# First-layer sums and stores handed out over the next pair, weight chunks asked for by ScalarE, one second-layer sum a step sooner, in a fused hash-attention and MLP kernel

## The chip, the cores and the metric

The kernel runs on one core of one Trainium2 chip. TensorE (PE) multiplies, VectorE (DVE), ScalarE (ACT) and GpSimd (POOL) do the rest, and SyncE (SP) mostly asks for transfers. The metric is the device time of the one core in microseconds (us), the median of a few runs. All sizes are fixed and all tensors float32 inside.

## The reference

Attention over buckets (a query sees the keys with the same six hash bits), followed by an MLP with a sigmoid GELU. What the change touches is the MLP alone.

```
q, k, v: (4, 8, 768, 64)   proj: (64, 6)   w_in: (512, 2048)   w_out: (2048, 512)
attn = softmax(where(bucket(q) == bucket(k), q k^T / 8, -1e9)) v
x = attn as (3072, 512)
h = x @ w_in
out = (h * sigmoid(1.702 h)) @ w_out
```

## The kernel before

**Stages.** Attention comes first (up to about 317 us of the profiled execution); it leaves `xT`, the transposed input of the MLP, in on-chip memory. Then comes the first layer (about 316 to 617 us), then the second (about 617 us to the end). Both layers are multiplied by a seven-product scheme: each operand is cut in 2 x 2 quarters, DVE and POOL form sums of the quarters (`sums_a` for the weights, `sums_b` for the data), PE makes seven products in place of eight, and the results are added up.

**First layer.** Tokens go in three blocks `sb` of 1024, features in eight tiles `mt` of 128 in each half, so there are 24 steps `n = 8 sb + mt`. One step makes four results of 128 features by 512 tokens, called `u`, `v`, `c21`, `c22`. A product (`product`, L740) is two multiplications by 128x128 weights over 512 columns; the trace shows each as two passes, so a product is "x4". Steps 0, 1, 20, 21, 22 and 23 run alone (`hidden`). Steps 2 to 19 run as nine pairs `t` (`pair_of_steps`), in which products 2 and 3 are themselves cut in seven smaller ones over 256 columns (`nested`, L801): PE makes a small product, DVE adds it to its result (L750), and the small products of one kind share a PSUM tile, so PE waits for DVE's addition before it goes on in that tile. The small products of the second kind (`third`) are left over to the start of the next pair (`behind`, `old`).

**What a step leaves.** ACT applies the GELU (`emit`, L747), and `g_outer` lets POOL form four sums of the results (L219 to L222 in `sums_b`; the second overwrites `v`). Seven tiles go to memory (`keep`, L744, 256 KB each: `c22`, `c21`, `u`, the overwritten `v` and the sums `t1`, `t2`, `t4`, which have one buffer each). In a pair, `g_outer` of both steps is called when the last nested results of the pair are done, that is after the product `p5(0)` of the next pair. In `hidden` it is called at the end of the step.

**Weights.** `w_out` comes as 64-bit numbers, and the chip makes float32 of them in chunks of 512 KB (`convert`): a transfer into `raw` (L162), six operations of DVE (L180, L182, L188, L193, L195, L198) and one of ACT (L190). `raw` has one buffer; L193 is its last reader. `conversions` strings 18 such chunks (two late ones of `w_in`, 16 of `w_out`) together; each call of `next(steps)` does one operation. `todo` gives each step of the first layer six calls, and in a pair they hang on the places 1 to 10 between the products (`hook`): the first step's at 1, 2, 2, 3, 3, 4, the second's at 6, 7, 7, 9, 9, 10.

**Order.** PE, DVE, ACT and POOL run their instructions in the order of the code (`ORDERED`). SP's order is made by a scheduler from the same code. All transfers before are asked for by SP, in one queue: one that waits for its data holds up all behind it. The instructions wait for each other by semaphores; a transfer also waits until the eighth one before it has landed.

**Second layer.** 21 steps of seven small products each, with `raw_g` or `s_in` as the data read back (L1013); DVE forms the sums for the next step (`later_sums`: L219, L220, L221, L222) at given places (`after(0)` to `after(4)`) of this one. At the step before the last another list is set at `after(3)`, which holds `later_sums[2:3]` too.

Of the kernel before, what the change touches and what calls it, by code (L numbers as in the profile page):

```python
# [8 lines left out]
F32 = mybir.dt.float32  # L9
# [10 lines left out]
P = 128  # L20
# [18 lines left out]
def kernel(  # L39
# [17 lines left out]
    nc = tc.nc  # L57
# [167 lines left out]
    XT = 512  # L225
# [469 lines left out]
    def feed_forward(tag, late=()):  # L695
# [9 lines left out]
        with ExitStack() as fctx:  # L705
# [12 lines left out]
            todo, turn = {}, [-1]  # L718
# [31 lines left out]
                nc.vector.tensor_tensor(dst, x, y, op=Alu.add)  # L750

            def g_outer(sb, mt, c11, c12, c21, c22):
                t1, t2, t4 = (stage.tile([P, XT], F32, tag=x, name=x, bufs=1) for x in ("t1", "t2", "t4"))
                for f, kept in zip(sums_b(nc.gpsimd, c11, c12, c21, c22, t1, t2, t4), ((4, t1), (1, c12), (5, t2), (6, t4))):
                    f()
                    keep(sb, mt, *kept)


            W = {}
# [69 lines left out]
            def pair_of_steps(t, mid):  # L829

                sb, m0 = divmod(2 * t, MT)
                mts = (m0, m0 + 1)
                a, b, u, v, c22, c21 = ([None, None] for _ in range(6))

                def p1(i):
                    a[i], u[i] = outer.tile([P, XT], F32, tag="a", name="product"), staged("u")
                    product(a[i], sb, mts[i], 1)
                    nc.scalar.copy(u[i], a[i])

                def p6(i):  # L840
                    product(a[i], sb, mts[i], 6, False)
                    v[i] = staged("v")
                    nc.scalar.copy(v[i], a[i])  # L843

                def p7(i):
                    product(a[i], sb, mts[i], 7, False)
                    c22[i] = staged("c22")
                    nc.scalar.copy(c22[i], a[i])

                def p5(i):  # L850
                    b[i] = outer.tile([P, XT], F32, tag="b", name="product")
                    product(b[i], sb, mts[i], 5)
                    add(v[i], b[i], v[i])

                def corner(i):
                    add(c22[i], b[i], c22[i])
                    emit(c22[i])
                    keep(sb, mts[i], 3, c22[i])

                def p4(i):  # L860
                    product(a[i], sb, mts[i], 4, False)
                    c21[i] = staged("c21")
                    emit(c21[i], a[i])
                    keep(sb, mts[i], 2, c21[i])

                def done2(i):
                    emit(u[i])
                    keep(sb, mts[i], 0, u[i])

                def done3(i):  # L870
                    emit(v[i])
                    if i == 0:
                        for j in range(2):
                            g_outer(sb, mts[j], u[j], v[j], c21[j], c22[j])

                def old():
                    if behind:
                        behind.pop(0)()

                def hook(at):  # L880
                    for f in mid.get(at, []):
                        f()

                p1(0)
                old()
                hook(1)
                p1(1)
                old()
                yield
                hook(2)  # L890
                p6(0)
                old()
                hook(3)
                p6(1)
                old()
                hook(4)
                p5(0)
                old()
                second = nested(2, sb, t, u, done2)
                second[0]()  # L900
                hook(5)
                p7(0)
                corner(0)
                second[1]()
                hook(6)
                p7(1)
                second[2]()
                hook(7)
                p5(1)
                corner(1)  # L910
                second[3]()
                hook(8)
                p4(0)
                second[4]()
                hook(9)
                p4(1)
                second[5]()
                third = nested(3, sb, t, v, done3)
                third[0]()
                behind.extend(third[1:])  # L920
                hook(10)

            heads = {}
# [7 lines left out]
            def hidden(sb, mt, mid=(), end=()):  # L931
                n = sb * MT + mt
                first = n not in heads
                nesting[0] = n < 2
                a, u = heads.pop(n) if n in heads else head(n)

                def old():
                    if behind:
                        behind.pop(0)()

                old()
                b = bank()
                if first:
                    product(b, sb, mt, 5)
                    old()
                product(a, sb, mt, 6, False)
                v, c21, c22 = (staged(x) for x in ("v", "c21", "c22"))
                nc.scalar.copy(v, a)
                if first:
                    old()  # L950
                    heads[n + 1] = head(n + 1)
                    old()
                else:
                    product(b, sb, mt, 5)
                product(a, sb, mt, 7, False)
                old()
                nc.scalar.copy(c22, a)
                add(c22, b, c22)
                emit(c22)
                keep(sb, mt, 3, c22)  # L960
                c = bank()
                product(c, sb, mt, 2)
                add(u, c, u)
                emit(u)
                keep(sb, mt, 0, u)
                if not first and n + 1 < n1 * MT and (n + 1) // 2 not in NESTED:
                    heads[n + 1] = head(n + 1)
                for x in mid:
                    x()
                product(a, sb, mt, 4, False)  # L970
                emit(c21, a)
                keep(sb, mt, 2, c21)
                product(b, sb, mt, 3, False)
                add(v, b, v)
                emit(v)
                g_outer(sb, mt, u, v, c21, c22)
                for x in end:
                    x()

# [114 lines left out]

            def conversions(cv, psum, chunks):

                gens = [convert(cv, *x, psum=psum) for x in chunks]
                next(gens[0])
                for i, x in enumerate(gens):
                    for y in gens[i + 1 : i + 2]:  # L1100
                        next(y)
                    for _ in x:
                        yield
                    yield

            def on(i, *fs):
                hooks[i] = hooks.get(i, []) + list(fs)
# [14 lines left out]
            order = [8 * k + 4 * c + i for c in range(2) for k in range(2) for i in range(4)]  # L1122
            chunks = [(w_out_sb[:, :, fc, :].rearrange("p r x -> p x r"), wo[fc]) for fc in order]
            steps = conversions(cv, cps, late + chunks)
            free = [i for i in range(LATE + 1, 3 * MT) if i % MT != MT - 1]
            for i in (list(range(1, LATE + 1)) if late else []) + free[:FC]:
                todo[i] = [lambda: next(steps)] * 6
# [13 lines left out]
                      [xT[:, k, XT * j : XT * (j + 1)] for k, j in ((2, 1), (0, 3), (1, 3), (1, 1))]]  # L1141
            places = [[x[:, j * TH : (j + 1) * TH] for x in y for j in range(2)] for y in places]
            more = nest_x(0, places[0])
            hidden(0, 1, nest_w(1) + more[2], more[3] + todo.pop(1, []))
            yield
            small_ctx.close()
            inner_ctx = fctx.enter_context(ExitStack())
# [2 lines left out]
            for t in NESTED:  # L1150
                sb, at = divmod(t, MT // 2)
                hooks = {}
                if at == 0:
                    on(1, x_sums[3], more[2][0])
                    for i, f in zip((2, 4, 5, 6, 7, 8, 9), more[2][1:] + more[3]):
                        on(i, f)
                for n, places_of in ((2 * t, (1, 2, 2, 3, 3, 4)), (2 * t + 1, (6, 7, 7, 9, 9, 10))):
                    x = todo.pop(n, [])
                    for i in places_of:
                        on(i, *x[:1])  # L1160
                        x = x[1:]
                    on(5 if n % 2 == 0 else 10, *x)
                if t + 1 < MT // 2:
                    on(5, *in_sums(t + 1))
                    on(8, *nest_w(t + 1))
                elif t + 1 == MT // 2:
                    on(5, *nest_w(0))
                if at == MT // 2 - 1:
                    x_sums = sums_b(nc.vector, *quarters_x(sb + 1))
                    more = nest_x(sb + 1, places[sb + 1])  # L1170
                    for i in range(3):
                        on(8 + i, x_sums[i])
                whole(pair_of_steps(t, hooks))
                yield
# [21 lines left out]
            for n, (sb, o) in enumerate(steps_out):  # L1196
# [11 lines left out]
                def after(at):  # L1208
# [1 line left out]
                        while pending:  # L1210
                            pending.pop(0)()

                    steps = [later_sums[at : at + 1]] if n == 0 else [[], later_sums[0:1], later_sums[1:2], later_sums[2:], []][at : at + 1]

                    if n + 2 >= len(steps_out):
                        turns = [lambda q=q: turned(m, int(final), int(not final), q, q + 1) for q in range(4)]
# [82 lines left out]
```

## Time and profile before

| | us |
|---|---|
| three runs | 884.53, 882.37, 883.58 (median 883.58) |
| profiled execution, its own time | 883.3 |
| its span from the first to the last instruction | 881.4 |
| PE busy | 855.8 |
| DVE busy | 709.9 |
| ACT busy | 340.6 |
| POOL busy | 330.8 |

The granted TensorE clock was 0.995 of full speed over the span. The page divides the span into 40 slices; PE is at 9 tenths or more in nearly all of them, so its few idle stretches have to be looked for one by one. In the timeline a row gives start, duration, engine, line, operation, output and inputs, and in brackets the idle time of that engine before it and what ended it. The list of waits gives, for an engine's line and what it waited for, the sum, the count and the longest. A view by windows gives each engine's busy time in each stretch.

### The profile page before, as it was taken

Reading aid. Unit: us, or ns where it says so; the run is one execution under the profiler, and the core shown is the slowest. Engines: PE = TensorE matmul, PEld = TensorE weight load, DVE = VectorE, ACT = ScalarE, POOL = GpSimd, SP = SyncE. Lnnn points to the kernel's source line nnn. Section 1 sums busy time; section 2 is a strip of 40 time slices with the busy share of each in tenths; the row PEclk is TensorE's granted clock in tenths of the full one; section 3 lists DMA queues with packets and bytes.
Section 4 is the critical chain, followed back from the end, with each engine's and each line's share of the span. In section 5 each row is a group of like instructions: output and inputs, shape, how many; then the busy total and the mean of one; then the engine's idle time right before and its main releaser. Section 6 shows DMA issues by size and latency. Waiting matters only on the chain.

```text
span 881.4 us, 13702 instructions
## 1 busy us (share of the span) xinstructions
PE 855.8 (97%) x4953; PEld 517.1 (59%) x4953; DVE 709.9 (81%) x1056; ACT 340.6 (39%) x567; POOL 330.8 (38%) x291
## 2 busy tenths in 40 slices
PE   9999999999999998999998899999999999999996
PEld 4444444444444443455554455544878888888885
DVE  4589999999999877767965687856797977897786
ACT  5866677766677632433333333333000000000000
POOL 4242243332234476377632254779913100000000
PEclk9999999999999999999999999999999999999998
DMA  6646644565542105354555555558745585477524
GB/s 132 95 62 106 94 83 84 102 115 98 94 82 81 35 21 194 120 176 146 199 184 171 198 192 191 177 205 310 246 184 191 177 226 215 155 225 237 196 99 99
DMA packets 169163, 132.12 MB, mean 150 GB/s; under 512 B 123616, under 2 KB 138112, under 8 KB 163712
## 3 DMA queue, kind: packets, MB, share of 16 engines
q1 hardware_dynamic: 166528, 129.70, 51.7%
q10 hardware_dynamic: 2560, 1.46, 0.7%
q8 instruction: 41, 0.67, 0.3%
q14 instruction: 34, 0.28, 0.1%
HBM read 79.69 MB, written 50.33 MB: 148 GB/s over the span
## 4 chain that ended last, share of the span: by engine, by line
PE 36%; issue 6%; DVE 5%; POOL 5%; DMA 1%; SPq 0%; ACT 0%; ACTq 0%; POOLq 0%; DVEq 0%
PE product L1058 26%; PE product L740 9%; PE small L801 2%; DVE xT L1062 1%; POOL t L222 1%; POOL t L221 1%; DMA raw<-in_moe_w_out_dram 1%; POOL t L219 1%; POOL v L220 1%; DVE v L750 1%; DVE y L1038 1%; DVE w_out_sb L195 0%; DVE v L1062 0%; DVE t2a L221 0%; DVE raw_g L220 0%
## 5 line engine op out<-in xcount | busy, mean ns | idle before, releaser
L433 ACT ACTIVATE e<-ps 128x768 f32<-128x768 f32 x192 | 151.2, 812 | 25.7 <-PE ps L432 23.1
L432 PE MATMUL ps<-qT,kT 64*128 64x384 f32 x768 | 155.1, 482 | 0.0
L465 PE MATMUL av<-e,v 128*32 128x385 f32 x1536 | 128.0, 487 | 0.0
L440 POOL TENSOR_TENSOR acc<-e 128x768 f32<-128x768 f32 x32 | 51.8, 1618 | 193.6 <-ACT e L433 174.1
L740 PE MATMUL product<-xT,w_in_sb 128*128 128x512 f32 x216 | 102.0, 602 | 3.6 <-ACT v L843 3.6
L465 PEld LDWEIGHTS av<-e,v 128*32 128x32 f32 x1536 | 48.6, 109 | 76.2 <-issue 74.5
L432 PEld LDWEIGHTS ps<-qT,kT 64*128 64x128 f32 x768 | 68.0, 187 | 38.5 <-issue 38.4
L740 PE MATMUL product<-t_x,s_in 128*128 128x512 f32 x192 | 89.4, 593 | 0.2 <-ACT u L928 0.2
L219 POOL TENSOR_TENSOR t<-v,u 128x512 f32<-128x512 f32 x24 | 33.6, 1399 | 110.9 <-ACT v L747 104.5
L1071 ACT COPY u<-product 128x256 f32<-128x256 f32 x21 | 7.8, 372 | 174.1 <-PE product L1058 140.8
L740 PEld LDWEIGHTS product<-xT,w_in_sb 128*128 128x128 f32 x216 | 41.3, 192 | 40.3 <-issue 33.7
L432 PE MATMUL ps<-qf,kf 64*128 64x384 bf16 x384 | 62.9, 324 | 0.1
L441 POOL TENSOR_TENSOR acc<-acc,e 128x768 f32<-128x768 f32 x32 | 55.8, 1744 | 2.5
L740 PEld LDWEIGHTS product<-t_x,s_in 128*128 128x128 f32 x192 | 36.3, 190 | 31.7 <-issue 27.5
L446 DVE SCALAR_TENSOR_TENSOR acc<-e 128x768 f32<-128x768 f32 x32 | 47.7, 1489 | 5.1 <-ACT e L433 5.1
L740 PE MATMUL product<-t_x,w_in_sb 128*128 128x512 f32 x96 | 45.3, 594 | 0.0
L432 PEld LDWEIGHTS <-kf 64*128 64x128 bf16 x384 | 18.9, 94 | 35.1 <-DMA q<-in_q_dram 6.2
L448 DVE TENSOR_TENSOR acc<-acc,e 128x768 f32<-128x768 f32 x32 | 34.3, 1072 | 3.3
L448 DVE TENSOR_TENSOR acc<-acc,acc 128x768 f32<-128x768 f32 x32 | 31.7, 991 | 6.3 <-POOL acc L441 3.2
L1058 PE MATMUL product<-raw_g,xT 128*128 128x256 f32 x152 | 35.1, 379 | 0.0
L221 POOL TENSOR_TENSOR t<-c,t 128x512 f32<-128x512 f32 x24 | 35.0, 1457 | 0.0
L222 POOL TENSOR_TENSOR t<-c,t 128x512 f32<-128x512 f32 x24 | 34.2, 1427 | 1.9
(241 smaller groups left out, 1636.9 us busy)
## 6 DMA issues: line engine op xcount, KB each, us to landing
raw_g<-g_dram SPq DMA_DIRECT2D x22, 1024.0 KB
s_in<-g_dram SPq DMA_DIRECT2D x20, 1024.0 KB
g_dram<-t SPq DMA_DIRECT2D x72, 256.0 KB
g_dram<-c SPq DMA_DIRECT2D x48, 256.0 KB
raw<-in_moe_w_in_dram SPq DMA_DIRECT2D x16, 512.0 KB
raw<-in_moe_w_out_dram SPq DMA_DIRECT2D x16, 512.0 KB
v<-in_v_dram SPq DMA_DIRECT2D x32, 192.0 KB
g_dram<-u SPq DMA_DIRECT2D x24, 256.0 KB
```

The lines of the kernel that those rows point to most:

```text
L219: return [lambda: eng.tensor_tensor(t1, b12, b11, op=Alu.subtract), lambda: eng.tensor_tensor(b12, b22, b12, op=Alu.subtract), lambda: eng ...
L221: lambda: eng.tensor_tensor(t2, b22, t1, op=Alu.subtract),
L222: lambda: eng.tensor_tensor(t4, b21, t2, op=Alu.subtract)]
L432: nc.tensor.matmul(ps[:, j, 0:HS], a[hs, keys], m[hs, cols], start=not last, stop=last)
L433: nc.scalar.activation(es[c][:, kt, :, 0:HS], ps[:, :, 0:HS], Act.Exp, scale=1.0 / D**0.5)
L440: nc.gpsimd.tensor_tensor(acc, es[c][:, 0, :, 0:HS], es[c][:, 1, :, 0:HS], op=Alu.add)
L441: nc.gpsimd.tensor_tensor(acc, acc, es[c][:, 2, :, 0:HS], op=Alu.add)
L446: nc.vector.scalar_tensor_tensor(acc, e[0], T * TINY, e[1], op0=Alu.add, op1=Alu.add)
L448: nc.vector.tensor_tensor(acc, acc, x, op=Alu.add)
L465: nc.tensor.matmul(av[D * j + d : D * j + d + 32, :], vt[:, t, j, d : d + 32], es[c][:, t, j, :], start=(t == 0), stop=(t == T - 1))
L740: nc.tensor.matmul(ps, wq[LEFT[i]][:, kc, :], xq[RIGHT[i]][:, kc, :], start=(start and kc == 0), stop=(kc == K2 - 1), skip_group_check=not ...
L1058: nc.tensor.matmul(ps, wq[LEFT[i]][:, c, :], gq[RIGHT[i]][:, c, :], start=(c == 0), stop=(c == F4 - 1))
```

## The change

Four things are edited.

1. In the first layer `g_outer` no longer runs the four sums and their stores at once: it puts four parts in a list, `outer_sums`, and `some(count)` runs that many of them. In a pair `some` stands behind the nested steps, 1, 2, 1, 2, 1 and 1 parts; in `hidden` all that is left runs before the fourth product, and the step's own four at its end. `c21` gets its buffer later in `hidden`.
2. The chunks are asked for with `queue=nc.scalar`, so by ScalarE, in its own order, and the request for the next chunk stands behind the fourth operation (L193) of this one.
3. In a pair the second step's six operations hang on 6, 7, 7, 7, 9, 9 in place of 6, 7, 7, 9, 9, 10; in step 1 four of the six stand before the fourth product.
4. In the second layer the third of `later_sums` (L221) moves from `after(3)` to `after(2)`.

```diff
             def g_outer(sb, mt, c11, c12, c21, c22):
-                t1, t2, t4 = (stage.tile([P, XT], F32, tag=x, name=x, bufs=1) for x in ("t1", "t2", "t4"))
-                for f, kept in zip(sums_b(nc.gpsimd, c11, c12, c21, c22, t1, t2, t4), ((4, t1), (1, c12), (5, t2), (6, t4))):
-                    f()
-                    keep(sb, mt, *kept)
+                t = {}
+                def part(i):
+                    if i != 1:
+                        t[i] = stage.tile([P, XT], F32, tag=f"t{i}", name=f"t{i}", bufs=1)
+                    sums_b(nc.gpsimd, c11, c12, c21, c22, t.get(0), t.get(2), t.get(3))[i]()
+                    keep(sb, mt, (4, 1, 5, 6)[i], t.get(i, c12))
+                outer_sums.extend(lambda i=i: part(i) for i in range(4))
+
+            outer_sums = []
+            def some(count):
+                for _ in range(count):
+                    if outer_sums:
+                        outer_sums.pop(0)()
...
                 second[0]()
+                some(1)
                 hook(5)
...
                 second[1]()
+                some(2)
                 hook(6)
...
                 second[2]()
+                some(1)
                 hook(7)
...
                 second[3]()
+                some(2)
                 hook(8)
...
                 second[4]()
+                some(1)
                 hook(9)
...
                 behind.extend(third[1:])
+                some(1)
                 hook(10)
...
-                v, c21, c22 = (staged(x) for x in ("v", "c21", "c22"))
+                v, c22 = staged("v"), staged("c22")
...
+                some(len(outer_sums))
                 for x in mid:
                     x()
+                c21 = staged("c21")
                 product(a, sb, mt, 4, False)
...
                 g_outer(sb, mt, u, v, c21, c22)
+                some(4)
...
-                gens = [convert(cv, *x, psum=psum) for x in chunks]
+                gens = [convert(cv, *x, queue=nc.scalar, psum=psum) for x in chunks]
                 next(gens[0])
+                yield
                 for i, x in enumerate(gens):
-                    for y in gens[i + 1 : i + 2]:
-                        next(y)
-                    for _ in x:
+                    for at in range(6):
+                        next(x, None)
+                        if at == 3 and i + 1 < len(gens):
+                            next(gens[i + 1])
                         yield
-                    yield
...
             steps = conversions(cv, cps, late + chunks)
+            next(steps)
...
-            hidden(0, 1, nest_w(1) + more[2], more[3] + todo.pop(1, []))
+            x = todo.pop(1, [])
+            hidden(0, 1, nest_w(1) + more[2] + x[:4], x[4:] + more[3])
...
-                for n, places_of in ((2 * t, (1, 2, 2, 3, 3, 4)), (2 * t + 1, (6, 7, 7, 9, 9, 10))):
+                for n, places_of in ((2 * t, (1, 2, 2, 3, 3, 4)), (2 * t + 1, (6, 7, 7, 7, 9, 9))):
...
-                    steps = [later_sums[at : at + 1]] if n == 0 else [[], later_sums[0:1], later_sums[1:2], later_sums[2:], []][at : at + 1]
+                    steps = [later_sums[at : at + 1]] if n == 0 else [[], later_sums[0:1], later_sums[1:3], later_sums[3:], []][at : at + 1]
```

## The prediction

> **What bounds the kernel now.** I read the page first: PE is nearly always busy, so only the places count at which it stands still.
>
> ```profile
> span 881.4 us, 13702 instructions
> PE 855.8 (97%) x4953; PEld 517.1 (59%) x4953; DVE 709.9 (81%) x1056; ACT 340.6 (39%) x567; POOL 330.8 (38%) x291
> ```
>
> The list of PE's waits from 300 to 700 us (the MLP) names them: line, what it waited for, us in total, times, longest.
>
> ```profile
> PE small L801 <- DVE v L750: 8.9, 9, 2.5
> PE product L740 <- ACT v L843: 3.6, 1, 3.6
> PE product L1058 <- DVE t2a L221: 1.7, 1, 1.7
> PE small L801 <- issue: 0.5, 1, 0.5
> ```
>
> That is nearly all there is: some 15 us. The first row is the pairs. Cut at the first `u` copy (L838) of each pair, the view by windows gives:
>
> ```profile
> 417.23:440.77 23.54, 23.27 (x69) 12.67 (x68) 22.23 (x40) 9.39 (x17) 16.77 (x17) 1.00 0.55 199
> 440.77:465.53 24.76, 23.98 (x69) 12.84 (x70) 17.34 (x31) 9.44 (x18) 10.06 (x8) 1.00 0.55 187
> 465.53:492.55 27.02, 23.81 (x69) 12.67 (x68) 16.73 (x30) 9.46 (x17) 10.07 (x8) 1.00 0.50 175
> 492.55:518.82 26.27, 23.81 (x69) 12.67 (x68) 16.18 (x27) 8.90 (x16) 11.25 (x8) 1.00 0.48 166
> ```
>
> (window, length, then busy us of PE, PEld, DVE, ACT, POOL.) The pair at 417 takes 23.54 us, though DVE has most to do in it; the seven pairs from 392.67 to 567.54 take 174.87 together, 10.1 more than seven times 23.54. What the slow ones share is in the timeline of SP, DVE and PE:
>
> ```profile
> 463.02 1.67 SPq L744 DMA_DIRECT2D g_dram<-t  x2
> 464.79 2.34 SPq L744 DMA_DIRECT2D g_dram<-c  x3
> 467.22 0.41 SPq L744 DMA_DIRECT2D g_dram<-u  x1
> 467.73 0.40 SPq L162 DMA_DIRECT2D raw<-in_moe_w_out_dram  x1
> 473.78 0.70 DVE L180 TENSOR_SCALAR part<-raw 128x512 uint32<-128x512 uint32 x1 [6.97 <-DMA raw<-in_moe_w_out_dram]
> 474.86 0.70 PE L801 MATMUL small<-xT,s_in 128*128 128x256 f32 x2 [2.49 <-DVE v L750]
> ```
>
> L193 had freed `raw` at 462.26, but the request stood in SP's queue behind the stores, and these behind POOL's sums (the last starts at 463.07): it left at 467.73 and landed about 473.8. DVE stood at L180 for 6.97 us, with the additions that PE's small products need behind it; PE lost 2.49 and, behind L193 and L195 in the same lag, 0.72 more. The pairs at 417 and 518 follow pairs with one chunk, whose load left early, and lose next to nothing inside.
>
> The second row of the waits is the same thing on ACT, ahead of the first chunk of the pairs:
>
> ```profile
> 333.92 1.35 DVE L506 TENSOR_TENSOR xT<-xT,rs 128x768 f32<-128x768 f32 x1
> 352.22 0.63 ACT L190 ACTIVATE size<-raw 128x512 f32<-128x512 f32 x1 [7.50 <-DMA raw<-in_moe_w_in_dram]
> 353.42 3.68 PE L740 MATMUL product<-xT,w_in_sb 128*128 128x512 f32 x4 [3.61 <-ACT v L843]
> ```
>
> **The change, part by part.**
>
> *Loads off SP's queue.* The request now follows L193 in ACT's order, so it leaves about 462.3 in place of 467.7, and in the odd steps L193 itself stands at place 7 in place of 9 (L180 began at 455.82 and L193 only at 461.57 in that pair, so some 3 us sooner). The load needs 4.0 to 4.5 us by itself (338.20 to 342.69, 348.13 to 352.16) and 6.05 beside stores (467.73 to 473.78), so it lands by 466.8, or 468.4 beside stores, and with the move some 3 us before that; the pair at 417 wants it 3.1 us after its `u` copy, which would be 468.6 here. So the 10.1 us go, but for what DVE's own lag keeps: in the two pairs with 22.2 and 22.7 us of DVE work the additions at the end still stand behind L195 and L198 (PE waited 0.27 at 440.41). I keep 0.5 for each of the two: **-9.1**. Bounds: -10.1 (nothing kept) and -7 (0.43 us, the whole delay at 440, in each of the seven).
>
> *The requests on ACT.* There are 18, each 0.37 to 0.42 us (ACT's own requests at the start and end of the span): 7.6 us on ACT, which is busy 8.9 to 9.6 us of a pair. The cover is ACT's idle time before each copy (1.6 us before the second `v` copy at 424.15); without it the cost is up to 7.6. But ACT also **waits** there, for L193. In a pair this wait stands in front of the second `v` copy: in the pair at 417, L193 ended at 424.21, the copy began at 424.15, and PE wants it only after `p5(0)`, two small products and `p7(0)`, 4 us later. Nothing is lost. At place 7 it holds up the GELU of `c22` and `c21`, which PE wants in the next pair: nothing either.
>
> *The same at the start.* Here it does cost. In the built program's order the first request stands between the GELU of `v` of step 0 and the `v` copy of step 1, and waits for DVE; the room of `raw` was the attention's, whose last user is L506, which ends at 335.27. So the copy that ran at 332.11 comes at 335.27 + 0.42 and takes 0.59: PE's next product, begun at 333.63, begins about 336.3, **+2.7**. The second request waits for L193 of the first chunk, in front of the GELU that reads the first step's last product (`c21`), and PE's second head needs that PSUM tile. DVE reaches L180 after L750 (337.26 + 2.7 = 340.0, 0.69) and L784 to L787 (2.35 by the rows from 337.87), at 343.0; four operations at 0.72 end at 345.9; request 0.42, GELU 0.60: 346.9. PE wanted the tile at 342.2 + 2.7 = 344.9: **+2.0**. In return the second chunk leaves at 346.3, lands about 350.5, and the 3.61 goes with 0.16 of pipeline refill: **-3.8**. Sum **+0.9**. Bounds: -1.8 (the first wait costs nothing) and +3.0 (L786 and L787 at 1.5 each, as at 342.29 beside POOL, and a wait as long as the 0.5 "issue" again).
>
> *Sums and stores handed out.* POOL has no cause to wait: its order holds almost the same instructions between the sums (only those for weights are set between them), so the eight sums still run together, 10.4 us from 453.97 to 464.35, as soon as ACT has made `v`. Only the stores' places in SP's queue move, and no load is behind them: 0. The cover is PE's distance to the tiles, which are wanted a whole pair later; if a store were late enough to hold up the single buffer of `t1`, POOL's next sum would be late, and then the copy that reuses the tile: bounded by the largest such wait of ACT on POOL or stores in this stage, 2.8 us, once.
>
> *One sum sooner.* At 646 PE waits for L221, and one addition of 0.33 (spacing of the rows 646.13 and 646.47) stands in front of it: **-0.3**, at most the whole 1.7. But the list for the step before the last still holds L221 at `after(3)`, so it now runs twice there; the built order of DVE shows both. The rows:
>
> ```profile
> 862.58 1.22 DVE L221 TENSOR_TENSOR t2a<-raw_g,t1a 128x1024 f32<-128x1024 f32 x1
> 864.08 1.89 PE L1058 MATMUL product<-t2a,s_in 128*128 128x256 f32 x8
> ```
>
> L221 ends at 863.80, and PE needs 0.14 behind it (647.68 to 647.82): it was ready 0.14 before its turn. A second one of 1.13 to 1.22 ends that much later: **+1.0**, and nothing after it hides a loss, since PE runs without a stop to the end. Bounds 0 and +1.3.
>
> Sum: -9.1 + 0.9 - 0.3 + 1.0 = **-7.5**. The profiled execution (883.3, span 881.4 and 1.9 around it) lies 0.3 below the median, so I take the difference from the median: 883.6 - 7.5 = **876.1**.
>
> **The rivals.**
>
> *The whole gain.* ACT is never held up at the start, and the gap at 646 closes as PE and DVE come in another phase: -10.1 - 1.8 - 1.7 + 1.0 = -12.6, **871.0**. For it: the pair at 417. Against: L506 is where it is.
>
> *POOL meets DVE.* Were the sums truly spread over the pair, they would meet more of DVE's own sums in the two full pairs. L786 takes 0.41 at 425.47 and 1.49 at 342.29, just as POOL's sums begin: 1.08 for a meeting. Each of these pairs has 12 such operations with both inputs on chip (L219 to L222, and L784 to L787 twice): 24 x 1.08 = 26 us. POOL is busy in 16.77 of 23.54 us there (71%), so that share is paid already, and the other 29%, 7.5 us, would be new: the whole gain, **883.6**, no change. Against: they already run beside each other from 412 to 420, and that pair is the fast one. The Trainium skill (SBUF — State Buffer, section "Who interferes with whom") says the port pair that VectorE shares with GpSimd is an exclusive lock that whoever comes first holds for the whole instruction; the trace's 0.41 and 1.49 fit it, and by it additions that read PSUM, as L750 in the pairs, with one input in SBUF, stay at 0.42.
>
> *ACT's waits decide (slower).* ACT stands in its order at each request until L193 is done, so a late DVE now also stops the copies that empty PSUM. It decides once a request costs PE more than 0.5 us on average: with 0.8 for the 15 that follow the first three, 12 us, -10.1 + 12 + 0.9 + 0.7 = +3.5: **887**. For it: 22.2 of 23.54 us of DVE in a full pair. Against: the 4 us of distance worked out above, and ACT's load of 40%.
>
> **How the numbers follow.** Chances: forecast 0.55 (its own range 873 to 880), the whole gain 0.2, POOL meets DVE 0.13, ACT's waits 0.12. Of the forecast and the whole gain nearly all is faster by over 0.3%, which is below 880.9 (0.3% is about what three runs, 882.4 to 884.5, can tell from no change): 0.76. Within: 0.13; slower: 0.11. The range from **871 to 884** takes the whole gain and the third case in and leaves out the last and what lies beyond the bounds.
>
> **What would show it.** Right: pairs of 23.3 to 24 us with no wait of L180 for `raw`; requests L162 on ACT right behind L193; a new PE wait of 2 to 3 us for ACT's L948 copy (step 1) and one of about 2 for the `c21` GELU; POOL's sums still in one run; L221 twice in the last but one step and PE about 1 us idle behind it. Wrong: pairs still over 24.5 us, ACT idle before `v` copies on DVE while PE waits, or POOL's sums torn apart by waits for stores.

## The result, and the profile after

The changed kernel takes **878.54 us** (median of six runs, 877.3 to 880.46), the kernel before 884.06 in its six (882.36 to 886.53): ratio 0.994, 95% interval 0.992 to 0.9961. At 884 us that is 5.3 us less (3.4 to 7.1). The forecast was 7.5 less. The profiled execution (879.71) is one of the two longer ones of the six, both with a mean granted clock of 0.993 where the others have 0.995 or 0.996.

The first lines of the page after: the span is 4.4 shorter, PE's busy time the same within 0.5, so it is again the idle stretches that count.

```profile
span 877.0 us, 13681 instructions
PE 855.3 (98%) x4953; PEld 518.9 (59%) x4953; DVE 711.8 (81%) x1057; ACT 339.5 (39%) x567; POOL 328.9 (38%) x291
```

The list of PE's waits from 300 to 700 us (line, what it waited for, us in total, times, longest):

```profile
PE product L740 <- ACT v L967: 2.6, 1, 2.6
PE small L814 <- DVE v L750: 2.5, 2, 1.4
PE small L814 <- issue: 2.4, 1, 2.4
PE product L1080 <- DVE t2a L221: 1.4, 1, 1.4
PE product L740 <- ACT c L747: 0.9, 1, 0.9
```

The 8.9 us in nine pieces that PE's small products lost to DVE's L750 are now 2.5 in two, and the 3.6 behind ACT's `v` copy in the first pair is gone. Three waits are new: 2.6, 2.4 and 0.9. All three stand at the start of the first layer, as the timeline of ACT, PE and DVE shows:

```profile
335.48 0.34 ACTq L162 DMA_DIRECT2D raw<-in_moe_w_in_dram  x1
335.86 0.58 ACT L967 COPY v<-product 128x512 f32<-128x512 f32 x1 [3.96 <-DVE xT L506]
336.50 5.32 PE L740 MATMUL product<-xT,w_in_sb 128*128 128x512 f32 x8 [2.55 <-ACT v L967]
346.87 0.33 ACTq L162 DMA_DIRECT2D raw<-in_moe_w_in_dram  x1
347.25 0.60 ACT L747 ACTIVATE c<-product 128x512 f32<-128x512 f32 x1 [3.50 <-PE product L740]
347.90 1.98 PE L740 MATMUL product<-xT,w_in_sb 128*128 128x512 f32 x4 [0.93 <-ACT c L747]
...
348.69 1.30 DVE L797 TENSOR_TENSOR w_out_sb<-xT 128x256 f32<-128x256 f32 x1
352.74 1.48 DVE L800 TENSOR_TENSOR w_out_sb<-xT,w_out_sb 128x256 f32<-128x256 f32 x1
359.04 0.41 DVE L750 TENSOR_TENSOR u<-small,u 128x256 f32<-128x256 f32 x1
359.55 0.67 PE L814 MATMUL small<-w_out_sb,w 128*128 128x256 f32 x2 [2.37 <-issue]
```

ACT stood at its first request until L506 was done, then made the `v` copy for which PE waited 2.55. The second request (346.87) stood in front of the GELU of `c21`: 0.93. For the third wait the profile names nothing ("issue"), but the PSUM tile says who: the second small product goes on in the tile that L750 reads, and L750 came at 359.04. DVE had had no idle time since 342.46. Four additions of 256 columns, which took 0.41 or 0.42 without POOL beside them (342.46 to 343.93), ran beside POOL's L219 to L222 (348.44 to 353.94), at 1.30 to 1.49 each, and the whole second chunk came behind them.

The view by windows, cut at the first `u` copy (L851) of each pair (window, length, then PE, PEld, DVE, ACT, POOL busy, granted clock):

```profile
396.34:419.55 23.21, 23.21 (x69) 12.92 (x68) 16.68 (x27) 9.04 (x16) 18.27 (x25) 1.00 0.52 182
419.55:444.65 25.10, 23.77 (x69) 12.50 (x68) 24.04 (x40) 9.14 (x17) 16.01 (x11) 1.00 0.67 232
444.65:468.04 23.39, 23.39 (x69) 13.09 (x70) 16.99 (x30) 9.34 (x18) 10.08 (x8) 1.00 0.57 195
468.04:491.25 23.21, 23.21 (x69) 12.92 (x68) 16.99 (x30) 9.35 (x17) 10.06 (x8) 1.00 0.60 207
```

Pairs that took 24.8, 27.0 and 26.3 now take 23.2 to 23.4 with PE busy in all of it, and nowhere does L180 wait for `raw`. Only the two pairs in which DVE has 23 to 24 us to do (419 and 514) take 25.1 and 24.9, and that is longer than before (23.5 and 24.4).

In the pair at 419 DVE is busy for 24.04 us with the same 40 operations that took 22.23 before. The first addition of the pair shows where 0.8 of it comes from (the rest comes with the places: in e12, where the sums are not handed out, it is 23.31). Before, it ran behind POOL's last sum:

```profile
419.73 0.67 DVE L784 TENSOR_TENSOR xT<-xT 128x256 f32<-128x256 f32 x1
```

In the changed kernel it runs beside one of the sums:

```profile
422.44 1.49 DVE L797 TENSOR_TENSOR xT<-xT 128x256 f32<-128x256 f32 x1
421.40 2.25 POOL L221 TENSOR_TENSOR t<-c,t 128x512 f32<-128x512 f32 x1
```

Handed out, the eight sums of this stretch are no longer in one run: POOL makes the sums for the next weights (408.52 to 412.34) between the first and the second of them, so that the last ends at 425.07, where it ended at 418.73 before.

Both traces hold 4953 matmuls in the same order up to the end, so the start of the same matmul in both says how far the changed kernel lags:

| matmul | before | after | lag | what came in between |
|---|---|---|---|---|
| eight passes ahead of it | 330.19 | 330.35 | +0.2 | the two executions start that far apart |
| step 1's product behind the `v` copy | 333.63 | 336.50 | +2.9 | wait for the `v` copy |
| its fifth pass | 335.35 | 339.94 | +4.6 | four passes at half the clock |
| second head | 342.21 | 347.90 | +5.7 | wait for the GELU of `c21` |
| last before the small products | 356.14 | 356.59 | +0.5 | the old 3.61 wait, and the half clock behind it, are gone |
| second small product | 357.58 | 359.55 | +2.0 | 2.37 where 0.49 was |
| five passes on | 360.24 | 363.90 | +3.7 | half the clock again |
| end of the last pair | 567.34 | 562.48 | -4.9 | the pairs: **-8.5** |
| second layer, step 1 | 647.82 | 642.63 | -5.2 | 1.36 where 1.70 was |
| after 690 | 696.52 | 691.05 | -5.5 | a gap of 0.11 ahead of this matmul is gone |
| last but one step | 864.08 | 859.43 | -4.7 | L221 twice: +0.9 |

So the pairs gave nearly what was expected, and the start took 3.5 of it back (from +0.2 to +3.7).

### The profile page after: what moved, and what is told of

Its sections match the earlier page's. It is cut to its first block, busy times and chain, and to the rows that moved or that the text cites. A ratio compares the mean times of both kernels' runs of the same rounds, so it can differ in the third digit from the quotient of the medians.

```text
span 877.0 us, 13681 instructions
## 1 busy us (share of the span) xinstructions
PE 855.3 (98%) x4953; PEld 518.9 (59%) x4953; DVE 711.8 (81%) x1057; ACT 339.5 (39%) x567; POOL 328.9 (38%) x291
## 4 chain that ended last, share of the span: by engine, by line
PE 87%; DVE 8%; issue 1%; ACT 1%; POOL 1%; DMA 1%; ACTq 0%; SPq 0%; DVEq 0%; POOLq 0%
PE product L1080 26%; PE product L740 22%; PE ps L432 17%; PE av L465 14%; PE small L814 5%; DVE xT L1084 1%; PE dn L486 1%; PE hash L408 1%; DVE v L750 1%; DMA q<-in_q_dram 1%; ACT e L433 1%; DVE y L1060 1%; DVE u L750 0%; DVE acc L448 0%; DVE t2a L221 0%
## 5 line engine op out<-in xcount | busy, mean ns | idle before, releaser
L433 ACT ACTIVATE e<-ps 128x768 f32<-128x768 f32 x192 | 151.2, 812 | 25.8 <-PE ps L432 23.2
L219 POOL TENSOR_TENSOR t<-v,u 128x512 f32<-128x512 f32 x24 | 34.5, 1436 | 112.0 <-ACT v L747 112.0
L750 DVE TENSOR_TENSOR v<-small,v 128x256 f32<-128x256 f32 x63 | 26.0, 418 | 22.6 <-PE small L814 22.3
L222 POOL TENSOR_TENSOR t<-c,t 128x512 f32<-128x512 f32 x24 | 35.2, 1468 | 1.9
```

What stands on the lines that cost most here:

```text
L222: lambda: eng.tensor_tensor(t4, b21, t2, op=Alu.subtract)]
L433: nc.scalar.activation(es[c][:, kt, :, 0:HS], ps[:, :, 0:HS], Act.Exp, scale=1.0 / D**0.5)
```

## The experiments

All kernels were timed beside the kernel before on the same chip; e1 to e4, e5 to e8 and e9 to e12 ran on three different chips, so rows are compared by their ratios. "us less" is one less the ratio, times 884. The first ten microseconds of the span differ by up to 2.6 us from one execution to another, so parts are compared by waits and by lags from 330 us on.

| kernel | us | ratio, 95% interval | us less |
|---|---|---|---|
| changed | 878.54 | 0.994 (0.992 to 0.9961) | 5.3 |
| e1: L221 once | 878.07 | 0.9922 (0.9907 to 0.9936) | 6.9 |
| e2: copy first | 875.17 | 0.9885 (0.987 to 0.99) | 10.2 |
| e3: additions later | 874.72 | 0.9883 (0.9867 to 0.9899) | 10.3 |
| e4: all four | 870.9 | 0.9836 (0.9822 to 0.9849) | 14.5 |
| e5: loads on SP | 878.7 | 0.9937 (0.9918 to 0.9957) | 5.6 |
| e6: sums at once | 878.19 | 0.9934 (0.9916 to 0.9953) | 5.8 |
| e7: old places | 876.83 | 0.9919 (0.99 to 0.9937) | 7.2 |
| e8: GELU first | 876.74 | 0.9918 (0.99 to 0.9937) | 7.2 |
| e9: place, request point | 877.05 | 0.9917 (0.9903 to 0.993) | 7.3 |
| e10: handing out alone | 889.12 | 1.0048 (1.0034 to 1.0062) | -4.2 |
| e11: all four, old places | 869.76 | 0.9828 (0.9815 to 0.9842) | 15.2 |
| e12: place alone | 876.61 | 0.9899 (0.9884 to 0.9914) | 8.9 |

**e1, the second L221.**

```diff
-                            steps = [later_sums[2:3], turns[0:2], turns[3:4], later_sums[3:], turns[2:3]]
+                            steps = [turns[0:2], turns[3:4], later_sums[3:], turns[2:3]]
```

> The changed kernel without the second L221 in the step before the last (its list at after(3) no longer holds later_sums[2:3]). Theory: that second addition is what PE waits for 0.74 us at 858.70, and the whole 0.8 us by which PE falls back there comes again: about 877.7, no PE wait at that place. Rival: another late input (stores, the next s_in) stands right behind it, and nothing is gained: 878.5.

The trace of the changed kernel near its end has L221 twice and PE's wait behind the second:

```profile
856.70 1.22 DVE L221 TENSOR_TENSOR t2a<-raw_g,t1a 128x1024 f32<-128x1024 f32 x1
858.17 1.21 DVE L221 TENSOR_TENSOR t2a<-raw_g,t1a 128x1024 f32<-128x1024 f32 x1
859.43 1.99 PE L1080 MATMUL product<-t2a,s_in 128*128 128x256 f32 x8 [0.73 <-DVE t2a L221]
```

Without it PE has no wait after 800 us at all, and the same matmul gains 0.9 on the ones ahead of it. The times alone (0.9922 and 0.994, intervals that overlap) could not have told this.

This run shows something else besides. The 2.55 us wait ahead of step 1's product is there again, but the passes behind it are at full speed. The views by windows give the granted clock as the first number behind POOL's busy time; first the changed kernel, then e1:

```profile
336.50:339.94 3.44, 3.44 (x5) 1.51 (x6) 0.00 (x0) 0.00 (x0) 3.20 (x7) 0.52 0.84 294
```

```profile
336.74:338.70 1.96, 1.95 (x5) 0.99 (x6) 0.00 (x0) 0.00 (x0) 1.80 (x4) 1.00 0.89 242
```

**e2, the `v` copy ahead of the first request.**

```diff
                 nc.scalar.copy(v, a)
+                for x in early:
+                    x()
...
-            next(steps)
...
-            hidden(0, 1, nest_w(1) + more[2] + x[:4], x[4:] + more[3])
+            hidden(0, 1, nest_w(1) + more[2] + x[:4], x[4:] + more[3], [lambda: next(steps)])
```

> The changed kernel with the first chunk's request on ACT set behind the v copy of step 1, not ahead of it. Theory A: ACT's wait for L506 is the cause of PE's 2.55 us wait at 333.95, and the granted clock of 0.55 to 0.59 behind that wait (1.7 us more for the next four matmuls) is its consequence; both go, DVE loses about 0.5 of it because the chunk lands no sooner (339.8): 874 to 874.5. Theory B: DVE's backlog up to 358 hangs on the chunks' landing, not on PE, so PE's wait at 357.18 grows from 2.4 to 5 or 6 and little is left: 877.5 to 878.5.

875.17, 4.9 less than the changed kernel by the ratios; the 2.55 is gone, the wait for the GELU of `c21` grew from 0.93 to 1.75, and the 2.37 stayed at 2.38. So theory A holds, though the time lies 0.7 above its range: DVE's backlog follows PE and does not stand still by the loads. By the traces 3.8 us of the difference arise at the start; another 1.0 arises in the second full pair, where PE's wait fell from 1.41 to 0.51, and why it fell no run here shows.

**e3, the four additions out of the backlog.**

```diff
-            hidden(0, 1, nest_w(1) + more[2] + x[:4], x[4:] + more[3])
+            hidden(0, 1, nest_w(1) + more[2] + x[:4], x[4:])
...
                 hooks = {}
+                if t == NESTED.start:
+                    for i, f in zip((5, 6, 7, 8), more[3]):
+                        on(i, f)
```

> The changed kernel with the four additions L797 to L800 that ran from 348.69 to 354.14 (1.3 to 1.5 us each beside POOL) moved out of step 1 into places 5 to 8 of the first pair. Theory: they are what makes DVE late for the first small product's addition; PE's 2.37 us wait at 357.18 falls to 0.5 or 1, and the four matmuls at half the granted clock behind it (360.7 to 363.9) run at full clock: 3 to 3.5 us faster, 875 to 875.5. Rival: the addition waits for ACT's v copy, which stands behind the third request (357.08) and so behind L193 of the second chunk; L193 still comes at 353 or so, the gain is the same wait less 1 us at most, 877.5.

874.72. The wait at 357 is gone altogether and so is the half clock behind it: the lag to the changed kernel goes from -0.1 to -4.4 in those 7 us and stays there. The four additions were the cause, and the `v` copy behind the third request was not.

**e8, the second request behind the GELUs.**

```diff
-            hidden(0, 1, nest_w(1) + more[2] + x[:4], x[4:] + more[3])
+            hidden(0, 1, nest_w(1) + more[2] + x[:3], x[3:] + more[3])
```

> The changed kernel with the second chunk's request behind the GELUs of c21 and v in ACT's order, not ahead of them (L193 of the first chunk then follows the v addition on DVE). Theory: PE's 0.93 us wait at 346.97 goes, the second chunk lands 0.7 later, which DVE's additions L797 to L800 cover: 877.5. Rival: the time goes into the wait at 357.18, which grows by as much: 878.5.

The 0.93 went, and 0.32 of it came back at the next wait (2.69 in place of 2.37). In this execution the passes behind that longer wait were at full clock (1.00), so the trace shows 2.5 less at that point; some 1.7 of it is the clock, which is not the edit's doing. The times alone (0.9918 and 0.994, intervals that overlap) do not show a gain.

**e4, the four edits together.**

> The three edits of the other runs together, and the second chunk's request behind the GELU of c21 (PE waited 0.93 for it). Theory: the four causes are separate and add up, -0.8 -4.1 -1.0 -3.3 = about -9: 869 to 870. Rival: the two waits at the start share one clock loss or one backlog, so at least 3 us of this are lost: 872.5 or more.

870.9, 0.9 above the theory's range and 1.6 below the rival's. The ratios of this run and of the changed kernel differ by 0.0104, or 9.2 us, as the theory's sum; by the traces it is 9.0, of which 8.3 arise at the start. The four single runs do not add up to it by their times (1.6, 4.9, 5.0 and 1.9 less, together 13.4): each is taken against the same changed kernel, whose interval is 1.8 us either way, and the half clock comes and goes from one execution to another. What is left at the start is 0.56 and 0.62, without a half clock behind.

**e5, the loads back on SP's queue.**

```diff
-                gens = [convert(cv, *x, queue=nc.scalar, psum=psum) for x in chunks]
+                gens = [convert(cv, *x, psum=psum) for x in chunks]
```

> The changed kernel with all 18 requests L162 back on SP's queue (convert without queue=nc.scalar), everything else as changed: handed-out sums and stores, place 7, later request points. Theory: the loads' queue is what the pairs gained by (8.5 us by PE's lag against the kernel before), so pairs of 25 to 27 us with L180 waiting for raw come back, while ACT's two waits at the start (4.6 and 1.1) go: 881 to 885. Rival: handing out the stores alone frees SP's queue, and the loads are in time on SP too; the start's loss goes and the pairs keep their gain: 873 to 875.

878.7: neither forecast. The start is other (waits of 1.72, 1.51 and 3.04), but the **pairs did not come back to 25 to 27**: they take 23.2 to 25.6, and from 364 us to the end the lag to the changed kernel moves by 0.1 in sum. The requests of the second chunk of a pair again left 3.3 to 6.1 us behind L193, and it cost PE next to nothing (0.05 and 0.06 outside the full pairs). The queue, to which the prediction gave the gain, is not needed for it.

**e6, the sums at once.**

```diff
-                outer_sums.extend(lambda i=i: part(i) for i in range(4))
+                for i in range(4):
+                    part(i)
```

> The changed kernel with the sums not handed out: the four parts of g_outer run where it is called, as before; the loads stay on ACT. Theory: POOL runs them in one burst either way and no load stands behind the stores any more, so handing out is worth nothing: 878 to 879. Rival: handing out spaces the stores or the sums so that they disturb the loads and DVE less: 880.5 or more without it.

878.19, the ratio 0.0006 from the changed kernel's: no difference that the times can show. With the loads on ACT, handing out is worth nothing. The traces show what it costs in one place: with the sums at once they end at 418.51 again, DVE is busy for 23.20 us in the first full pair in place of 24.04, and the pair takes 24.41 in place of 25.10.

**e7, the old places.**

```diff
-                for n, places_of in (..., (2 * t + 1, (6, 7, 7, 7, 9, 9))):
+                for n, places_of in (..., (2 * t + 1, (6, 7, 7, 9, 9, 10))):
```

> The changed kernel with the odd steps' chunk operations back at places (6, 7, 7, 9, 9, 10), so that L193 and with it the next request come some 3 us later in each pair. Theory: the load has 3 us to spare, so the time stays within 1 us: 878 to 879.5. Rival: it lands too late for L180 at place 1 or 2 in the pairs, DVE waits again 2 to 3 us there: 882 or more.

876.83, not slower. L180 waits for `raw` twice (0.8 and 1.4) and runs 4.5 and 4.7 us after the request there, and PE's waits in the pairs are 0.22 and 0.58. The two full pairs shrink to 24.56 and 23.37. The place is not needed either, if the loads are on ACT. Which of the two is enough, alone, the next three runs ask.

**e9, loads on SP and sums at once: the place and the request point are left.** The edits of e5 and e6 together.

> The changed kernel with the loads on SP's queue and the sums not handed out: of the three things that were to cure the pairs, only the earlier place of L193 (7 in place of 9) is left, with the request asked for right behind L193. Theory: each of the three is enough by itself, since L193 3 us sooner lets the load land 3 us sooner behind the same queue; L180 may wait up to 3 us for raw but PE's longest wait for it stays under 1: as with the loads on SP and handed-out sums, 878 to 879.5. Rival: SP's queue needs one of the other two; the requests lag 5 us behind L193 and PE loses 0.7 to 2.5 us in four pairs again: 882 to 885.

877.05. The requests lag 5.1 to 5.8 us behind L193, no less than before (1.8 to 5.5), DVE waits up to 3.7 us for `raw`, and yet the pairs gain 9.5.

**e12, the kernel before with the new places alone** (but for `c21`'s buffer, which is taken later in `hidden`, and those of the sums, which are taken one by one).

```diff
-                for n, places_of in (..., (2 * t + 1, (6, 7, 7, 9, 9, 10))):
+                for n, places_of in (..., (2 * t + 1, (6, 7, 7, 7, 9, 9))):
```

> The kernel before with nothing but the odd steps' places (6, 7, 7, 7, 9, 9), so that L193 comes sooner; loads on SP, sums at once, the first two chunks as before. Theory: L193 3 us sooner is enough by itself to bring the loads in time: the pairs win 6.5 to 8.5 us, and the start loses nothing: 875.5 to 877.5. Rival: the requests still stand behind the stores of POOL's burst, which ends when it ended before; they leave when they left before, and nothing is won: 883 to 885.

876.61: 8.9 us less from one number, more than the whole change. The lag to the kernel before moves by 9.0 in the pairs and not at all at the start. The timeline of SP and DVE shows how, in the pair that answers to the one at 465 before:

```profile
463.20 1.68 SPq L744 DMA_DIRECT2D g_dram<-t  x2
464.97 0.38 SPq L744 DMA_DIRECT2D g_dram<-c  x1
465.45 0.40 SPq L162 DMA_DIRECT2D raw<-in_moe_w_out_dram  x1
465.95 0.93 SPq L744 DMA_DIRECT2D g_dram<-c  x2
471.11 0.69 DVE L180 TENSOR_SCALAR part<-raw 128x512 uint32<-128x512 uint32 x1 [3.35 <-DMA raw<-in_moe_w_out_dram]
```

The pair's `u` copy is at 466.46. The request still stands behind the stores of POOL's sums, 5.05 us behind L193. But SP's scheduler now set it two `c` stores and a `u` store further ahead: it leaves 1.0 us before the `u` copy, where it left 2.2 after it, and L180 runs 4.65 us after that copy in place of 8.25. DVE stands idle for 3.35 us and PE loses next to nothing (pair 23.42). The first half of the cause, a load some 3 us too late, was right. That the queue had to be changed for it was not. (The pairs with most to do for DVE take 24.45 and 24.89 here.)

**e10, handing out alone.** The kernel before with the first edit only.

> The kernel before with nothing but the sums and their stores handed out over the next pair (loads on SP with their old request point, old places, old list in the second layer). Theory: the request now stands among the stores and not behind them all, so it lags 3.3 to 3.9 us behind L193 in place of 4.8 to 5.5, some 1.5 us in four pairs, and PE wins about that: 880 to 881 (kernel before 884). Rival 1: it wins nothing, since POOL's burst still holds the store ahead of the request: 883.5 to 885. Rival 2: it is worth the whole gain of the pairs, 8.5: 875.5.

889.12: **slower by 4.2**, outside all three forecasts. The timeline of POOL, SP and PE in the third pair:

```profile
399.70 1.27 POOL L221 TENSOR_TENSOR t<-c,t 128x512 f32<-128x512 f32 x1
401.00 0.33 SPq L744 DMA_DIRECT2D g_dram<-t  x1
402.39 0.40 SPq L162 DMA_DIRECT2D raw<-in_moe_w_out_dram  x1
408.11 1.22 PE L814 MATMUL small<-w_out_sb,s_in 128*128 128x256 f32 x2 [5.68 <-DVE v L750]
```

L193 had freed `raw` at 392.33. But the last handed-out sums now stood on POOL behind the sums for the next weights (396.14 to 399.75), their store waited for them, and the request stood in SP's queue behind the store: 10.06 us late. PE lost 5.68 there, and ran behind it at half the clock (0.50 from 408.1 to 413). So handing out, by itself, harms; it is the loads on ACT (e7), or the earlier place (e5), that take the harm away.

**e11, the combined run with the old places.**

> The four edits of the combined run together with the old places (6, 7, 7, 9, 9, 10), which had taken 2.0 us off PE's waits at 431 to 444 and 538. Theory: the two are in different stages and add up: 868.5 to 869.5. Rival: with PE 8 us ahead the loads land too late for the old places, and it comes out as the combined run or slower: 871 or more.

869.76, which the interval does not tell from e4's 870.9. In its trace the places take PE's waits in the full pairs from 1.07 and 1.41 to 0.56 and 0.94. Both beat the kernel before and the changed one.

## Why the prediction was right, and where it was wrong

- **What bounds, and the way of the time**: right. The pairs lost their time to chunks that landed late, and gained 8.5 (forecast 9.1). That the size fits so well is in part luck: two misses nearly cancel. The forecast gave 23.54 to each pair and 0.5 more to each of the two full ones. The five others came out at 23.2 to 23.4, 1.4 better in sum, and the two full ones at 25.1 and 24.9, 1.9 worse.
- **Loads off SP's queue**: the size right, the credit wrong. The step added two causes, 5.4 us of queue and 3 of place, and took both for needed. e12 shows that the place alone does it (e5 and e9 agree), e7 that the loads on ACT do it with the old places; the loads on ACT without the sums handed out were not run with the old places. They are substitutes, so the edit had one gain, not two halves. The loads on ACT cost no copy inside the pairs, as forecast: e5 and the changed kernel gain the same there in sum (8.6 and 8.5).
- **The start** (+0.9 forecast, +3.5 measured) is the step that failed. The first wait was exact (a wait of 2.55, by which the lag grew 2.7, as forecast); the second was 0.93, not 2.0, since the first four additions ran free of POOL. But "the 3.61 goes, -3.8" didn't ask what DVE does with a chunk that is there earlier: the four additions and the second chunk became a backlog for which PE waited 2.37. And no term had the clock: 1.7 us behind the new wait and 1.7 behind the backlog, against 1.4 that the old wait had cost.
- **Sums and stores handed out: 0**: right for this change by the times (e6), and POOL's sums still run in one burst in most pairs (455.78 to 466.2 in the fifth). But not in all: "only those for weights are set between them" was enough to tear them apart in the third pair and to make the fourth 0.7 us longer (e6). And the reason, that no load is behind the stores, is the work of another edit; without that cover it is a loss of 4.2 (e10), more than the bound of 2.8 that was given.
- **One sum sooner**: -0.3 forecast, the wait went from 1.70 to 1.36. **L221 twice**: +1.0 forecast, 0.73 of wait and 0.9 of lag; e1 shows that nothing else stands behind it.
- **Rivals**: the whole gain fell by the start. "POOL meets DVE" was right at two places, the four additions at 348.69 and the full pair at 419, where DVE's work grew by 1.8 us and the pair by 1.6, of which 0.8 and 0.7 go with the sums handed out (e6). The 7.5 us of that rival were far too many: handing out brought DVE and POOL together anew in one pair only. ACT's waits cost PE 3.5 us at the start and nothing in the pairs.

## What to carry to other kernels

Where several edits of one change all bring the same load forward, price each alone: one of them may do all of it, and the others may cost. When a wait goes, follow the engine that had been waiting: the work it now does sooner, and beside whom, is the next wait. An edit worth nothing because another covers it should be written down with the cover's name; here it would have cost 4.2 us by itself.

## What was not expected of the hardware

A stop of PE has a price behind it that is not the same each time. The same 2.55 us wait ahead of step 1's product stands in six traces. Behind it the granted clock was 0.52 to 0.57 over the next 3.4 to 4 us, 1.7 us lost at most, in four of them (the changed kernel, e3, e7, e8), and 1.00 in two (e1, e6).

The 14 traces show what decides. In the MLP every stretch of half clock is 3.41 us long, or twice that, and within one trace they start whole multiples of 3.41 us apart: 336.38 and 360.27 in the changed kernel (seven of them), 355.52, 406.72 and 485.23 in e10 (15 and 23). Cut every trace on that grid; for e4 and e11, which have no half clock before PE's last matmul, the half clock behind it gives the grid. Then add up PE's idle time in each stretch of 3.41 us:

| stretch | PE idle in it | granted clock in the next |
|---|---|---|
| before, 472.91 (part of the 2.49 wait) | 1.94 | 1.00 |
| e2, 353.28 (part of the 2.38 wait) | 2.05 | 0.50 |
| changed kernel, 332.97 (nearly all of the 2.55 wait) | 2.43 | 0.50 |
| e1, 331.80 and 335.21 (the 2.55 wait, cut in two) | 1.02 and 1.54 | 1.00 and 1.00 |
| e6, 332.27 and 335.69 (the same) | 1.40 and 1.15 | 1.00 and 1.00 |
| e8, 353.84 and 357.25 (the 2.69 wait, cut in two) | 1.41 and 1.28 | 1.00 and 1.00 |

In all 14 traces half clock followed each of the 16 stretches at full clock in which PE was idle for 2.05 us or more, and none with 1.94 us or less. (At half clock less was enough to keep it there: 1.30 and 1.39 us in e10.) So what decides is how much of a wait falls into one stretch of the grid. The grid does not lie the same way in each execution, which is why the same wait goes both ways.

The Trainium skill (TensorE: Matmul & The Clock Gate, section "Part 1: The HAM clock gate (the "warmup" mystery)") says that the clock falls to half after at least one idle window of about 3.4 us, and that the window runs freely. The length and the free run agree with these traces. But a window need not be idle from end to end: 2.05 of its 3.41 us were enough, so 3.4 us is no safe limit for a wait.
